# Last dV store but one over fifteen DMA engines, results by GpSimd, second dV written in one go

## The chip, the cores and the metric

The kernel runs on one core of a Trainium2 chip. The core has five engines that run side by side: TensorE (PE; its weight loads are listed apart as PEld), VectorE (DVE), ScalarE (ACT), GpSimd (POOL) and SyncE (SP, which here only issues DMAs). Sixteen DMA engines move data between the main memory (HBM) and the on-chip memory (SBUF, 128 partitions). SP, ACT and GpSimd can each issue DMAs; each has its own queue, and all of them are served by the same sixteen DMA engines. The metric is device time in microseconds (us) of one execution: 644.63 us, the median of three (643.6 to 645.44).

## The reference

One decoding step of attention and its gradient. There are 32 heads; each has one query row, 8192 key rows and 8192 value rows of 128 numbers, all bfloat16.

```
scores = einsum('bhqd,bhkd->bhqk', q, k) * D**-0.5
attn   = softmax(scores)
out    = einsum('bhqk,bhkd->bhqd', attn, v)
```

The outputs are `out` and, by the vector-Jacobian product with `grad_out`, dq, dk and dv. With one query row, dV is the outer product of the softmax weights p and the row of `grad_out`; dK is the outer product of ds = scale · p · (V·grad_out − sum) and the row q. So K and V are read once (67 MB each), and dK and dV, as large as they are, are written: 134.23 MB read and 134.23 MB written by the profile. `out` and dq are 8 KB each.

## The kernel before, in words

**Tiles.** The 32 heads go in `HP` = 16 pairs, t = 0 to 15. One pair's K (or V) is a tile of 128 partitions by 128 rows of 128 numbers, 32 KB a partition, 4 MB in all. There are three buffers for K (`Kt`, K[t] in buffer t mod 3) and two for V (`Vt`). dK and dV are written in place over K and V (`outer`, L325, on DVE: eight operations per tile, one for each eighth of the rows) and are then stored from there (`store`, L335, always issued by SP). A load into a buffer can therefore start only when the store out of it has landed.

**Loads and stores.** `load` (L78 to L81) and `store` (L335 to L339) issue on SP's queue, in program order. A transfer of 4 MB is one DMA of 128 rows of 32 KB, eight rows for each of the sixteen DMA engines. The first and last tiles are moved in quarters or halves.

**Scores of K.** `k_block(t, c)` (L181) takes one eighth of K[t]: DVE transposes it in 32 by 32 blocks (L184), PE multiplies it by the query's columns (L192). Eight blocks make the scores of one pair; DVE and ACT make the softmax of them (`s_back`, `s_top`, `s_exp`, `p_of`).

**Scores of V.** `v_part(t, m)` transposes V on PE (L253), ACT copies it out (L259), `v_scores` multiplies (L270).

**The order.** The program is written out by hand (`tc.manual_schedule()`): every engine executes its instructions in the order in which the Python calls come. The loop over t at L373 does in each pass, in this order on DVE: the dK of pair t−1 (`dk`, eight outer products, stored when done), with the softmax of pair t between them; then the dV of pair t (`outer(t, "p", r)`, r = 0 to 7). From r = 3 on, one block of K of the next pair follows each outer product (L445 to L450). After r = 7 dV is stored (L452; for the first and the last pair in quarters, L447), then come the three last K blocks with the first parts of V (L453 to L456), the load of K[t+2] (L460) and of V[t+2] (L462). At t = 16 only the dK of pair 15 is left, stored in quarters.

**The results.** After the loop `result` (L341) transposes `out` and dq on PE, copies them on ACT and stores each with one DMA of 32 rows of 256 bytes, issued by ACT (L348).

**Semaphores of the DMAs.** Each DMA signals its landing on one of eight semaphores (100, 102, 103, 104, 105, 108, 109 and 110 in the trace), which are handed out in turn to the DMAs of SP and ACT together. Before a DMA takes a semaphore whose last user went through other work, its queue waits until that user has landed. Near the end the turn was: V[14]'s store 103, the first result 104, the first half of dK[14] 105, the second result 108, the second half of dK[14] 109, the four quarters of dV[15] 110, 100, 102 and 103, and the four quarters of dK[15] 104, 105, 108 and 109.

Of the kernel before, what the change touches and what calls it, by code (L numbers as in the profile page):

```python
# [11 lines left out]
BF16 = mybir.dt.bfloat16  # L12
F32 = mybir.dt.float32
# [14 lines left out]
def kernel(  # L28
# [11 lines left out]
    nc = tc.nc  # L40
    P = 128
    _, H, S, D = k.shape
    HP = H // 2
    NT = 2 * S // P
# [15 lines left out]
    small = ctx.enter_context(tc.tile_pool(name="small", bufs=2))  # L60
# [12 lines left out]
    Vt = {t: v_in[t % V_BUFS] for t in range(HP)}  # L73

    def rows_of(x, t, a, b):
        return x[0, 2 * t:2 * t + 2].rearrange("h s d -> (h s) d").rearrange("(p n) d -> p n d", p=P)[:, a:b, :]
# [6 lines left out]
    def load_k(t, parts=1):  # L83
        load(k, Kt, t, parts)
# [96 lines left out]
    def k_block(t, c):  # L181
        x = st[t]
        X = xkpool.tile([P, BN, NW, QD], F32, tag="XK", name="XK_sb")
        nc.vector.transpose(X[:], Kt[t][:, c * BN:(c + 1) * BN, :].rearrange("p n d -> p (n d)").bitcast(F32).rearrange(  # L184
            "p (n w j) -> p n w j", n=BN, w=NW))
        if c == 0:
            x["s"] = psS.tile([P, 512], F32, tag="s", name="s_ps")
        cols = X[:].rearrange("p n w i -> p (n w i)").bitcast(BF16).rearrange(
            "p (n w i e) -> p w e n i", n=BN, w=NW, e=2)
        for w in range(NW):  # L190
            for e2 in range(2):
                nc.tensor.matmul(x["s"][:], lhsT=q_win[:, 2 * w + e2, SL - 1 - c:SL - 1 - c + P],  # L192
                                 rhs=cols[:, w, e2], start=(c == 0 and w == 0 and e2 == 0),
                                 stop=(c == NB - 1 and w == NW - 1 and e2 == 1), skip_group_check=True)

    def s_back(t):
        x = st[t]
        x["sT"] = backs.tile([P, BN, QD], F32, tag="back", name="sT")
        nc.vector.transpose(x["sT"][:].rearrange("p n r -> p (n r)"), x.pop("s")[:])  # L199

    def s_top(t):
        x = st[t]
        mx = small.tile([P, 1], F32, tag="mx")
        nc.vector.reduce_max(mx[:], x["sT"][:, :, 0:NB], axis=AX.XY)
        top = small.tile([P, 1], F32, tag="top")
        nc.vector.tensor_scalar_mul(top[:], mx[:], scale)
        nc.tensor.transpose(x["m"][:, 128:256], top[:].to_broadcast([P, P]), ident_f[:])  # L207

    def s_exp(t):
        x = st[t]  # L210
        nbias = small.tile([P, 1], F32, tag="nbias")
        for s in range(2):
            a, b = s * HF, (s + 1) * HF
            nc.vector.tensor_reduce(nbias[a:b], x["m"][a:b, 128 + a:128 + b], axis=AX.X, op=ALU.max, negate=True)
        e = x["e"] = single.tile([P, NT], F32, tag="e", name="e")
        rs = small.tile([P, 1], F32, tag="rs")
        nc.scalar.activation(e[:].rearrange("p (c n) -> p n c", c=NB), x["sT"][:, :, 0:NB], ACT.Exp, bias=nbias[:],
                             scale=scale, accum_out=rs[:])
        return rs

    def s_sum(t, rs):
        nc.tensor.matmul(st[t]["m"][:, 0:1], lhsT=same[:], rhs=rs[:], start=True, stop=True, skip_group_check=True)  # L222
# [38 lines left out]
    def v_scores(t, z):  # L261
        x = st[t]
        cols = x.pop(("XV", z)).rearrange("p m s -> p (m s)").bitcast(BF16).rearrange(
            "p (m s e) -> p e m s", s=P, e=2)
        if z == 0:
            x["dp"] = psD.tile([P, 512], F32, tag="dp", name="dp_ps")
        at = SL - 2 - 2 * z
        for e2 in range(2):
            for b in range(NQ):
                nc.tensor.matmul(x["dp"][b * QD:(b + 1) * QD, :], lhsT=do_win[:, b // 2, e2, at:at + QD],  # L270
                                 rhs=cols[:, e2, :, b * QD:(b + 1) * QD],
                                 start=(z == 0 and e2 == 0), stop=(z == NZ - 1 and e2 == 1), skip_group_check=True)
# [52 lines left out]
    def outer(t, which, r):  # L325
        x = st[t]
        X, row = (Kt[t], 0) if which == "ds" else (Vt[t], 1)
        a, b = r * BN, (r + 1) * BN
        nc.vector.tensor_tensor(  # L329
            X[:, a:b, :].rearrange("p n (a b) -> p n a b", b=R),  # L330
            x[which][:, a:b, :].unsqueeze(2).to_broadcast([P, BN, D // R, R]),
            x["qd"][:, row, :].rearrange("p (a b) -> p a b", b=R).unsqueeze(1).to_broadcast([P, BN, D // R, R]),
            op=ALU.mult)

    def store(t, which, parts=1, last=None):  # L335
        X, dst = (Kt[t], out_2) if which == "ds" else (Vt[t], out_3)
        L = NT // parts
        for c in (range(parts) if last is None else (last,)):
            nc.sync.dma_start(rows_of(dst, t, c * L, (c + 1) * L), X[:, c * L:(c + 1) * L, :])  # L339

    def result(src, dst):  # L341
        half = single.tile([P, H], BF16, tag="ds1", name="half")
        nc.scalar.copy(half[:], src[:])
        fin_ps = psT.tile([P, 2 * TB, P], BF16, tag="T", name="fin_ps")
        nc.tensor.transpose(fin_ps[0:H, 0, :], half[:], ident[:])
        fin_sb = small.tile([H, D], BF16, tag="qd", name="fin_sb")
        nc.scalar.copy(fin_sb[:], fin_ps[0:H, 0, :])
        nc.scalar.dma_start(dst.rearrange("b h s d -> (b h s) d"), fin_sb[:])  # L348

    NV = NZ * NM // TB  # L350

    def v_part(t, m):
        v_bank(t, m)
        v_copy(t, m)

    HALF = NB // 2
# [16 lines left out]
    for t in range(HP + 1):  # L373
        o = t - 1
        now, old = t < HP, t > 0
        parts = 4 if o == HP - 1 else 2 if o == HP - 2 else 1

        def dk(a, b):
            for r in range(a, b if old else a):
                outer(o, "ds", r)  # L380
                if (r + 1) % (NB // parts) == 0:
                    store(o, "ds", parts, r * parts // NB)

        dk(0, 2)
        if now:
            if old:
                v_part(t, 3)
                v_part(t, 4)
            s_back(t)
            s_top(t)  # L390
            if old:
                v_scores(t, 0)
                v_part(t, 5)
                v_part(t, 6)
        dk(2, 3)
        if now:
            rs = s_exp(t)
            if old:
                for m in (7, 8, 9):
                    v_bank(t, m)  # L400
            s_sum(t, rs)
            if old:
                v_copy(t, 7)
                v_copy(t, 8)
        dk(3, 4)
        if now:
            p_of(t)
            if old:
                v_copy(t, 9)
                v_scores(t, 1)  # L410
                v_part(t, 10)
                v_part(t, 11)
                contract(t, "p")
                v_part(t, 12)
                v_part(t, 13)
                v_scores(t, 2)
                v_part(t, 14)
                v_part(t, 15)
                v_scores(t, 3)
            else:  # L420
                contract(t, "p")
            if old and t + 1 < HP:
                weights_do(t + 1)
        dk(4, NB)
        if not now:
            break
        fine = t == 0 or t == HP - 1
        outer(t, "p", 0)
        outer(t, "p", 1)
        if fine:  # L430
            store(t, "p", 4, 0)
        v_back(t)
        pd_sum(t)
        if t % ST == 0 and old:
            gather(o, "ds")
        outer(t, "p", 2)
        ds_of(t)
        contract(t, "ds")
        if t % ST == ST - 1:
            gather(t, "p")  # L440
        if t + 1 < HP:
            prepare(t + 1)
        else:
            gather(t, "ds")
        for r in range(3, NB):  # L445
            outer(t, "p", r)
            if fine and r % 2:  # L447
                store(t, "p", 4, r // 2)
            if t + 1 < HP and r >= HALF - 1:
                k_block(t + 1, r - HALF + 1)  # L450
        if not fine:
            store(t, "p")  # L452
        if t + 1 < HP:  # L453
            for c in range(HALF + 1, NB):
                k_block(t + 1, c)
                v_part(t + 1, c - HALF - 1)  # L456
            if t + 2 < HP:
                weights_q(t + 2)
        if 0 < t and t + 2 < HP:
            load_k(t + 2)  # L460
        if t + 2 < HP:
            load_v(t + 2, 4 if t == 0 else 1)  # L462
# [34 lines left out]
```

## Time and profile before

| what | value |
|---|---|
| median of three runs | 644.63 us (643.6 to 645.44) |
| the profiled execution's own time | 645.34 us |
| its span, first to last instruction | 643.5 us |
| DVE busy | 503.4 us, 78% |
| PE busy | 448.9 us, 70% |
| ACT busy | 196.0 us, 30% |
| POOL busy | 4.4 us, ten instructions, all before 5 us |
| DMA, SP's queue (q1) | 268.45 MB, 98.1% of sixteen engines' span |
| mean rate over the span | 418 GB/s |
| issue to landing of 4 MB: K load, V load, dK store, dV store | 19.9, 19.3, 29.0, 20.8 us |

The span is cut into 40 slices of 16.1 us on the page. In the sixth slice (80 to 97 us) the rate is 320 GB/s, in the first 353 and in the last two 373 and 269; in the others from the seventh on it lies between 411 and 440 GB/s. The trace also keeps one record for each packet of a DMA and sixteen landing marks for each DMA, one from each DMA engine. It doesn't say which of the sixteen engines a mark or a packet belongs to.

POOL issues no DMA in this kernel.

### The profile page before, as it was taken

The numbers are of one execution on the slowest core, as the hardware profiler recorded it, in microseconds if no ns is written. First come the engines' busy times: TensorE is split into PE (matmuls) and PEld (weight loads), VectorE is DVE, ScalarE is ACT, GpSimd is POOL, SyncE is SP. The second block draws the span as 40 slices with busy tenths as digits, with TensorE's granted clock in tenths as the row PEclk, the third lists the DMA queues.
The fourth block names the chain that finished last, engine by engine and source line by source line (L and its number), as shares of the span: only waits on it lengthen the run. The fifth ranks groups of instructions, "written<-read, shape, count | busy, mean of one in ns | idle before, by whom it ended". The sixth has DMA issues, their size and how long they took to land.

```text
span 643.5 us, 8005 instructions
## 1 busy us (share of the span) xinstructions
PE 448.9 (70%) x3256; PEld 240.5 (37%) x3256; DVE 503.4 (78%) x608; ACT 196.0 (30%) x456; POOL 4.4 (1%) x10
## 2 busy tenths in 40 slices
PE   6768777776868577585785948759687594874840
PEld 6225343442525234153351513416344161431530
DVE  3688999978969599595986959868597695977991
ACT  6113333340604206052060521505215060240610
POOL 2000000000000000000000000000000000000000
PEclk9868798876959779696797987858689695887965
DMA  8999979999999999999999999999999999999986
GB/s 353 431 446 395 439 320 422 420 425 438 435 423 436 429 432 426 430 433 433 428 429 440 428 427 434 431 415 431 417 436 425 431 423 418 437 429 411 424 373 269
DMA packets 12180, 268.97 MB, mean 418 GB/s; under 512 B 1520, under 2 KB 1520, under 8 KB 1520
## 3 DMA queue, kind: packets, MB, share of 16 engines
q1 hardware_dynamic: 12000, 268.45, 98.1%
q8 instruction: 25, 0.41, 0.2%
q14 instruction: 11, 0.09, 0.0%
q10 hardware_dynamic: 144, 0.02, 0.0%
HBM read 134.23 MB, written 134.23 MB: 417 GB/s over the span
## 4 chain that ended last, share of the span: by engine, by line
DMA 44%; DVE 27%; PE 12%; issue 10%; ACT 3%; SPq 1%; DVEq 0%; ACTq 0%
DMA K<-in_k_dram 37%; DVE XK_sb L184 17%; DVE K L329 5%; DMA out_dram<-K 5%; PE T_ps L253 4%; PE s_ps L192 4%; DVE V L329 3%; DMA out_dram<-V 3%; ACT XV_sb L259 2%; PE dp_ps L270 2%; DVE sT L199 1%; PE acc_p L309 1%; PE m_ps L207 1%; SPq L81 1%; ACT p_rep L235 0%
## 5 line engine op out<-in xcount | busy, mean ns | idle before, releaser
L192 PE MATMUL s_ps<-XK_sb,q_win 128*128 128x512 bf16 x512 | 170.7, 471 | 94.8 <-DVE XK_sb L184 93.7
L184 DVE STREAM_TRANSPOSE XK_sb<-K 128x1024 f32<-128x1024 f32 x128 | 152.8, 1223 | 91.3 <-DMA K<-in_k_dram 91.0
L259 ACT COPY XV_sb<-T_ps 128x512 f32<-128x512 f32 x240 | 130.3, 590 | 285.1 <-PE T_ps L253 284.7
L329 DVE TENSOR_TENSOR V<-p_rep,qd 128x2048 bf16<-128x2048 bf16 x128 | 152.1, 1201 | 2.0 <-PE acc_p L309 2.0
L329 DVE TENSOR_TENSOR K<-ds_rep,qd 128x2048 bf16<-128x2048 bf16 x128 | 149.9, 1213 | 0.5
L253 PE MATMUL T_ps<-ident_f,V 128*128 128x128 f32 x1024 | 137.0, 281 | 0.0
L253 PEld LDWEIGHTS T_ps<-ident_f,V 128*128 128x128 f32 x1024 | 116.0, 143 | 38.1 <-issue 9.8
L192 PEld LDWEIGHTS <-q_win 128*128 128x128 bf16 x512 | 57.3, 113 | 191.5 <-issue 167.5
L309 PE MATMUL acc_ds<-K,win_ds 128*32 128x512 bf16 x512 | 55.1, 606 | 27.7 <-ACT win_ds L228 27.7
L270 PE MATMUL dp_ps<-XV_sb,do_win 128*32 128x512 bf16 x480 | 37.2, 383 | 12.6 <-ACT XV_sb L259 11.6
L309 PEld LDWEIGHTS <-win_ds 128*32 128x32 bf16 x512 | 17.2, 134 | 52.5 <-ACT win_ds L228 27.1
L309 PE MATMUL acc_p<-V,win_p 128*32 128x512 bf16 x512 | 32.3, 396 | 3.7 <-ACT win_p L228 1.9
L170 ACT CAST qd<-m_ps 128x256 bf16<-128x256 f32 x16 | 6.0, 372 | 48.3 <-PE m_ps L166 48.1
L228 ACT COPY win_ds<-ds 64x128 bf16<-64x128 bf16 x32 | 9.5, 296 | 36.1 <-DVE ds L296 35.9
L309 PEld LDWEIGHTS <-win_p 128*32 128x32 bf16 x512 | 12.7, 99 | 18.6 <-ACT win_p L228 5.4
L289 PE MATMUL m_ps<-pd,same 128*128 128x1 f32 x32 | 6.2, 264 | 18.7 <-DVE m_ps L283 18.7
L270 PEld LDWEIGHTS <-do_win 128*32 128x32 bf16 x512 | 11.0, 94 | 19.8 <-issue 16.4
L280 DVE STREAM_TRANSPOSE dpT<-dp_ps 128x512 f32<-128x512 f32 x16 | 11.5, 717 | 4.8 <-PE dp_ps L270 4.8
L289 PEld LDWEIGHTS m_ps<-pd,same 128*128 128x128 f32 x32 | 4.9, 191 | 27.1 <-DVE m_ps L283 27.1
L199 DVE STREAM_TRANSPOSE sT<-s_ps 128x512 f32<-128x512 f32 x16 | 11.4, 711 | 4.4 <-PE s_ps L192 4.4
L233 DVE RECIPROCAL rinv<-m_ps 128x1 f32<-128x1 f32 x16 | 2.7, 168 | 13.7 <-PE m_ps L222 13.7
L235 ACT ACTIVATE p_rep<-e,rinv 128x512 bf16<-128x512 f32 x16 | 11.9, 746 | 0.9 <-DVE rinv L233 0.9
(61 smaller groups left out, 158.7 us busy)
## 6 DMA issues: line engine op xcount, KB each, us to landing
K<-in_k_dram SPq DMA_DIRECT2D x15, 4096.0 KB, 19.9
V<-in_v_dram SPq DMA_DIRECT2D x14, 4096.0 KB, 19.3
out_dram<-K SPq DMA_DIRECT2D x14, 4096.0 KB, 29.0
out_dram<-V SPq DMA_DIRECT2D x14, 4096.0 KB, 20.8
V<-in_v_dram SPq DMA_DIRECT2D x8, 1024.0 KB, 9.7
out_dram<-V SPq DMA_DIRECT2D x8, 1024.0 KB, 14.5
K<-in_k_dram SPq DMA_DIRECT2D x4, 1024.0 KB, 16.3
out_dram<-K SPq DMA_DIRECT2D x2, 2048.0 KB, 14.7
```

Source lines behind the costliest of these rows:

```text
L184: nc.vector.transpose(X[:], Kt[t][:, c * BN:(c + 1) * BN, :].rearrange("p n d -> p (n d)").bitcast(F32).rearrange("p (n w j) -> p n w j", ...
L192: nc.tensor.matmul(x["s"][:], lhsT=q_win[:, 2 * w + e2, SL - 1 - c:SL - 1 - c + P], rhs=cols[:, w, e2], start=(c == 0 and w == 0 and e2 == 0),
L199: nc.vector.transpose(x["sT"][:].rearrange("p n r -> p (n r)"), x.pop("s")[:])
L228: nc.scalar.copy(win[which][a:b, :, at + 4 * s:at + 4 * s + 4], src[a:b].rearrange("p (g j) -> p g j", j=4))
L235: nc.scalar.activation(x["p"][:], x["e"][:].unsqueeze(2).to_broadcast([P, NT, R]), ACT.Copy, scale=rinv[:])
L253: nc.tensor.transpose(T_ps[:, j, :], words[:, at * P:(at + 1) * P], ident_f[:])
L259: nc.scalar.copy(x["XV", z][:, i * TB:(i + 1) * TB, :], x.pop(("T", m))[:])
L270: nc.tensor.matmul(x["dp"][b * QD:(b + 1) * QD, :], lhsT=do_win[:, b // 2, e2, at:at + QD], rhs=cols[:, e2, :, b * QD:(b + 1) * QD], start ...
L280: nc.vector.transpose(dpT[:].rearrange("p m r -> p (m r)"), x.pop("dp")[:])
L289: nc.tensor.matmul(x["m"][:, 1:2], lhsT=same[:], rhs=x["pd"][:], start=True, stop=True, skip_group_check=True)
L309: nc.tensor.matmul(acc[which][b * QD:(b + 1) * QD, :], lhsT=win[which][:, g, at:at + QD], rhs=X[:, 4 * g:4 * g + 4, :].rearrange("p n d -> ...
L329: nc.vector.tensor_tensor(X[:, a:b, :].rearrange("p n (a b) -> p n a b", b=R), x[which][:, a:b, :].unsqueeze(2).to_broadcast([P, BN, D // ...
```

## The change

Three edits:

1. dV[14], the last pair but one, is stored by `store_spread`. GpSimd first issues a tiny DMA of five rows (`turn`, two numbers a row, into a small tile that nothing reads) and then one DMA of the partitions 0 to 119, 120 rows of 32 KB. SP issues the partitions 120 to 127 as two DMAs of four rows. The name of the change says that the 120 rows go over fifteen DMA engines, and that the tiny DMA turns the cursor from which GpSimd's DMAs are dealt out.
2. The two results are issued by GpSimd instead of ACT.
3. In the pass t = 1 no K block stands between the outer products of dV[1]; all eight outer products come first, then dV[1]'s store, then the blocks 0 to 4 of K[2], and then blocks 5 to 7 as before.

```
+    def store_spread(t):
+
+        turn = small.tile([P, 1], F32, tag="mx", name="turn")
+        nc.gpsimd.dma_start(turn[0:5].bitcast(BF16).unsqueeze(2), q[0, 0:5].rearrange("h s d -> (h s) d")[:, 0:4].rearrange(
+            "h (a b) -> h a b", b=2)[:, :, 0:1])
+        nc.gpsimd.dma_start(rows_of(out_3, t, 0, NT)[0:120], Vt[t][0:120], max_dma_last_dim=16384)
+        for a in (120, 124):
+            nc.sync.dma_start(rows_of(out_3, t, 0, NT)[a:a + 4], Vt[t][a:a + 4])
+
     def result(src, dst):
...
-        nc.scalar.dma_start(dst.rearrange("b h s d -> (b h s) d"), fin_sb[:])
+        nc.gpsimd.dma_start(dst.rearrange("b h s d -> (b h s) d"), fin_sb[:])
...
-            if t + 1 < HP and r >= HALF - 1:
+            if t + 1 < HP and t != 1 and r >= HALF - 1:
                 k_block(t + 1, r - HALF + 1)
-        if not fine:
+        if t == HP - 2:
+            store_spread(t)
+        elif not fine:
             store(t, "p")
+        if t == 1:
+            for c in range(HALF + 1):
+                k_block(t + 1, c)
         if t + 1 < HP:
             for c in range(HALF + 1, NB):
                 k_block(t + 1, c)
```

## The prediction

> **What bounds the kernel now.** I read the DMA rows first, then SP's queue in time, then windows, and last the landing marks.
>
> ```profile
> q1 hardware_dynamic: 12000, 268.45, 98.1%
> q8 instruction: 25, 0.41, 0.2%
> 523.37 0.34 SPq L81 DMA_DIRECT2D K<-in_k_dram  x1
> 563.02 0.34 SPq L81 DMA_DIRECT2D K<-in_k_dram  x1
> 592.07 0.34 SPq L339 DMA_DIRECT2D out_dram<-V  x1
> 602.74 6.31 SPq L339 DMA_DIRECT2D out_dram<-K  x2
> 610.99 9.43 SPq L339 DMA_DIRECT2D out_dram<-V  x4
> 627.68 5.80 SPq L339 DMA_DIRECT2D out_dram<-K  x4
> ```
>
> Columns of the lower rows are start, duration, queue, line and transfer. The DMA engines (I call each a lane) are busy 98.1% of the span, so compute is under cover and only lane time counts. A packet of 32 KB takes 1.21 us (median of the packet records), so eight packets, one lane's share of 4 MB, take 9.7 us and the four transfers of a pair 38.7. The K loads come 39.65 us apart. The missing 0.93 us is the second row: 25 packets of 16 KB of the program itself, 1.5 per pair, each worth half a 32 KB packet, 0.61 us; 1.5 × 0.61 = 0.92. That fits only if one lane gets them all. The landing marks say the same: of the sixteen marks of one DMA the last is 1.7 us behind the median for K[1]'s load (landed 34.5 us) and 6.7 us for V[14]'s store (median 606.2, fifteenth 607.9, sixteenth 612.9). Since loads wait for the slow lane's landing, the other lanes cannot run further ahead, and from some 400 us on the slow lane sets the pace. Its sum: after 85 us 56 shares of 4 MB are left (64 less eight), 56 × 9.7 = 543, plus 22 × 0.61 = 13, together 556 us; from 85.1 to its last landing at 642.66 are 557.5. It is never idle.
>
> ```profile
> 82.00:84.50 2.50, 1.04 (x4) 0.38 (x4) 2.50 (x3) 0.00 (x0) 0.00 (x0) 1.00 0.06 26
> 84.50:85.10 0.60, 0.00 (x0) 0.00 (x0) 0.60 (x1) 0.00 (x0) 0.00 (x0) 1.00 0.00 0
> 624.00:627.50 3.50, 0.00 (x0) 0.00 (x0) 3.50 (x4) 0.00 (x0) 0.00 (x0) 0.50 0.47 197
> 627.50:630.50 3.00, 0.00 (x0) 0.00 (x0) 1.64 (x2) 0.26 (x1) 0.00 (x0) 0.50 0.73 300
> 638.80:642.30 3.50, 0.00 (x0) 0.00 (x0) 0.00 (x0) 0.00 (x0) 0.00 (x0) 0.50 0.06 26
> ```
>
> The last two numbers of a window are the DMA share and GB/s. 0.06 is one lane of sixteen: in the last 3.5 us a single lane works. Around 625 us the fifteen others starve, and from 82 to 85 us all do.
>
> ```profile
> SPq L339 <- DMA out_dram<-fin_sb: 11.3, 2, 7.2
> 627.69 0.26 ACT L347 COPY fin_sb<-fin_ps 32x128 bf16<-32x128 bf16 x1 [4.31 <-DMA out_dram<-fin_sb]
> ```
>
> SP waited for the results' landings before it stored dK[15]: the first quarter shares semaphore 104 with the first result (landed 627.62), the third 108 with the second (632.59).
>
> **Second dV in one go.** dV[1]'s last product ends at 84.2 us because four blocks stand between the products.
>
> ```profile
> 75.12 1.24 DVE L184 STREAM_TRANSPOSE XK_sb<-K 128x1024 f32<-128x1024 f32 x1
> 77.39 1.24 DVE L184 STREAM_TRANSPOSE XK_sb<-K 128x1024 f32<-128x1024 f32 x1
> 79.65 1.24 DVE L184 STREAM_TRANSPOSE XK_sb<-K 128x1024 f32<-128x1024 f32 x1
> 81.91 1.24 DVE L184 STREAM_TRANSPOSE XK_sb<-K 128x1024 f32<-128x1024 f32 x1
> ```
>
> Each costs 1.13 us of pitch, so the store leaves SP 4.5 us earlier, 79.8 instead of 84.28, before dK[0]'s store has left any lane (first lane 81.7, slow lane 84.5 by the packet records). The slow lane then saves its idle time from 84.5 to the first packet at 85.1 to 85.3: **0.7 us**. The others save some 3.5 us, which are lost again, as they may not run ahead. Behind the store in SP's queue stands K[3]'s load, which needs dK[0]'s landing at 84.9 and went at 84.97; it stays. The moved blocks end at the same 88.7 on DVE; PE takes 1.03 us for a block's four products (83.20 row: 1.04), less than DVE's 1.13, so it ends some 1 us after DVE as before. Cost zero, under cover of K[2]'s later work; without the cover a microsecond.
>
> **dV[14] off the slow lane.** The transfer's size is unchanged. If the lane left out is the slow one, its work shrinks by eight packets, 9.7 us: 642.66 − 0.7 − 9.7 = 632.3, and it no longer ends last. No row names the slow lane, so the relief lies between 0 and 9.7 us; I take 9.7, since its marks make it the one lane for which fifteen-lane dealing makes sense at all, and keep 0 as a rival. SP's eight rows are eight packets; two DMAs of four rows put one packet each on at most four lanes, twice: between 0.6 (spread evenly, 9.7/16) and 2.4 us (2 × 1.21) more on some lanes. I take 2.4, four rows being unable to reach more than four lanes at a packet a row.
>
> GpSimd's issue has no row. SP's takes 0.85 us from issue (84.28) to first packet (85.12). The store leaves DVE at 592.07 and the first lane is done with what stands before it (dK[13], first mark) at 595.8, so up to 3.7 us are hidden; beyond that each microsecond is one lost. I take zero; the far end is the rival below. The tiny DMA is ten numbers; it waits only for an old buffer of the row maximum, free since pair 13's softmax, so it stands ahead of the store by tens of microseconds. On POOL's queue nothing else waits; on SP's, dK[14]'s first half is behind the two small stores, 2 × 0.34 us, and went 10 us later anyway. Nobody waits for dV[14]'s landing but the end.
>
> **Results by GpSimd.** The two result DMAs leave the turn of eight semaphores, the extra small store enters it. By the turn, dK[15]'s quarters then follow users that land by 618 us, so they leave SP when DVE has made them: products at 619.98 in steps of 1.14, so 622.3, 624.6, 626.9 and 629.1 instead of 627.68 to 633.07. ACT's second copy waits for the first result (4.3 us), off the path: the second result may land as late as 636. For the slow lane alone this part is worth nothing (it was never starved); with the slow lane relieved it is worth the 3.5 us that the fifteen others starve.
>
> **Sum.** dV[15]'s last quarter lands on the fifteen lanes at 625.0 to 627.4, median 625.8. Shifted by 0.7: 624.3 to 626.7. Four quarters of dK[15] without a gap, 4 × 2.44 = 9.8. The four lanes with two more rows: 2.4. So these end at 636.5 to 638.9 by where they stand among the fifteen; I take 638.0, over the middle because the latest of four counts. Compute does not bind: the last quarter leaves at 628.4 and needs 3.3. The last landing moves by 642.66 − 638.0 = 4.7. The profiled execution took 645.34 (span 643.5 and 1.84 around it), 0.71 above the median; 645.34 − 4.7 = 640.6, so **640.0** by the median of 644.63. Own range 638.4 to 641.0.
>
> **Rivals.**
> - The lane left out is not the slow one: all lanes but it are as before, only 0.7 us is won: 643.9. For it: the trace names no lane, and a cursor can stand elsewhere. Against it: nothing in rows. If the slow lane is even one of the four with two more rows: 643.9 + 2.4 = 646.3. Chances 0.15 and 0.04. [...]
> - The other side: the GpSimd store itself is slow, through late issue, or because rows taken in blocks of eight, and four rows next to each other, crowd one way out of SBUF. Price: nothing up to a second 9.7 us on fifteen lanes (pace halved), or up to 2 × 3 × 1.21 = 7.3 on four (four packets one after the other instead of at once). It decides at 4.7 us, where the gain is gone: 644.6; at the far end 640.0 + 9.7 = 649.7. For it: every transfer that runs at 430 GB/s here has 128 rows on all lanes; no row shows another. Against it: a lane works on two queues at once (the 16 KB program packets took 0.95 us beside data), so dK[13] and dK[14], in the other queue, fill what a slow packet leaves. Chance 0.20: 0.07 of it so that the end lies within 0.3% of before, 0.13 slower. [...]
>
> **Chances.** As forecast 0.61. 0.3% (1.9 us) is about what a measurement of this kernel can tell from none. Faster: 0.61. Within: 0.15 + 0.04 + 0.07 = 0.26. Slower: 0.13. The range from 638.3 to 646.3 leaves out the slow store's far end and little else.
>
> **What would show it.** Right: the store of dV[1] leaves SP at 79.8 and the window 82 to 85 us has a DMA share near 1; dK[15]'s quarters leave at 621.6 to 628.4; at the end no window of share 0.06, and the sixteenth mark of dK[15] is within 3 us of the median. Wrong: one lane still alone for 3 us at the end (another lane freed); marks of the GpSimd store or the small ones 10 us and more behind their turn (slow store); SP still waiting for results.

## The result and the profile after

The changed kernel takes 649.8 us (median of 4 runs, 649.13 to 650.29) against 644.12 us for the kernel before on the same chip: ratio 1.0086, 95% interval 1.0064 to 1.0107, so 5.7 us slower. I had forecast 640.0 in a range of 638.3 to 646.3. The profiled execution took 649.72 us, its span 647.9.

First the DMA queues of the changed kernel by the page (packets, MB, share of sixteen engines' span), SP's queue and POOL in time, and one row of the DMA issues between 588 and 626 us (size, us to landing):

```profile
q1 hardware_dynamic: 11872, 264.52, 96.4%
q0 software_dynamic: 368, 3.95, 2.0%
...
588.07 1.13 SPq L348 DMA_DIRECT2D out_dram<-V  x2
598.73 6.34 SPq L339 DMA_DIRECT2D out_dram<-K  x2
606.99 10.74 SPq L339 DMA_DIRECT2D out_dram<-V  x4
618.36 9.34 SPq L339 DMA_DIRECT2D out_dram<-K  x4
...
588.35 0.77 POOL L346 DMA_DIRECT2D out_dram<-V  x1 [70.68 <-DVE V L329]
...
out_dram<-V POOLq DMA_DIRECT2D x1, 3840.0 KB, 35.6
```

GpSimd's queue is q0. Its 240 data packets of 16 KB (the 120 rows came out as two packets each) took 0.84 us in the mean of the packet records, together the 2.0% of 16 × 647.9 us; the 256 packets of 16 KB of dK[14]'s halves took 0.61 in the kernel before (median). The store needed 35.6 us to land, where SP's store of the whole tile took 20.8 before. Everything up to it was early: dV[14] left at 588.07 instead of 592.07, and the first quarter of dK[15] at 618.36 instead of 627.68. These nine microseconds of head start were lost between there and the end.

Windows, with the DMA share and GB/s as the last two numbers, show where. The first line is the kernel before, the others are the changed kernel:

```profile
602.00:624.00 22.00, 15.61 (x146) 10.07 (x143) 20.59 (x25) 9.67 (x25) 0.00 (x0) 0.81 0.99 422
...
82.00:84.50 2.50, 2.50 (x8) 0.87 (x7) 1.80 (x3) 0.00 (x0) 0.00 (x0) 0.63 1.00 433
...
592.00:600.00 8.00, 7.27 (x63) 5.21 (x61) 6.90 (x12) 5.15 (x12) 0.00 (x0) 1.00 0.90 255
600.00:612.00 12.00, 8.14 (x97) 4.56 (x94) 11.58 (x16) 6.18 (x14) 0.00 (x0) 0.90 1.01 311
612.00:624.00 12.00, 6.48 (x42) 4.29 (x34) 12.00 (x12) 1.41 (x6) 0.53 (x1) 0.50 0.99 389
624.00:636.00 12.00, 0.00 (x0) 0.00 (x0) 1.14 (x2) 0.25 (x1) 0.52 (x1) 0.50 0.96 401
636.00:640.00 4.00, 0.00 (x0) 0.00 (x0) 0.00 (x0) 0.00 (x0) 0.00 (x0) 0.50 0.64 270
640.00:643.00 3.00, 0.00 (x0) 0.00 (x0) 0.00 (x0) 0.00 (x0) 0.00 (x0) 0.50 0.27 112
643.00:646.40 3.40, 0.00 (x0) 0.00 (x0) 0.00 (x0) 0.00 (x0) 0.00 (x0) 0.50 0.13 53
```

The row from 82 us is the stretch that stood at a share of 0.06 before; it is full now. From 592 to 612 us the lanes are as busy as ever (0.90 and 1.01) but move 255 and 311 GB/s. Against the 422 GB/s of the first line that is 8 × 167 + 12 × 111 + 12 × 33 = 3064 KB less by 624 us (1 GB/s times 1 us is 1 KB), or 7.3 us of DMA time. The end is ragged: in the last 3.4 us the share is 0.13, two lanes. The sixteen landing marks of dK[15]'s last quarter run from 631.25 to 646.92. The sign of a slow store that the prediction named is there: the GpSimd store landed 35.6 us after its issue, 15 us more than SP's.

### The profile page after: what moved, and what is told of

Same layout as the page of the kernel before. It is cut to its first block, busy times and chain, and to the rows that moved or that the text cites. A ratio compares the mean times of both kernels' runs of the same rounds, so it can differ in the third digit from the quotient of the medians.

```text
span 647.9 us, 8009 instructions
## 1 busy us (share of the span) xinstructions
PE 440.1 (68%) x3256; PEld 236.8 (37%) x3256; DVE 503.6 (78%) x608; ACT 195.7 (30%) x456; POOL 6.9 (1%) x14
## 4 chain that ended last, share of the span: by engine, by line
DMA 45%; DVE 26%; issue 11%; PE 11%; ACT 4%; SPq 1%; POOLq 0%; POOL 0%; DVEq 0%; ACTq 0%
DMA K<-in_k_dram 36%; DVE XK_sb L184 16%; DMA out_dram<-K 8%; DVE K L329 4%; PE T_ps L253 4%; PE s_ps L192 3%; DVE V L329 3%; ACT XV_sb L259 2%; PE dp_ps L270 2%; DVE sT L199 1%; PE acc_p L309 1%; PE m_ps L207 1%; ACT p_rep L235 1%; PE m_ps L321 1%; PE acc_ds L309 1%
## 5 line engine op out<-in xcount | busy, mean ns | idle before, releaser
L192 PE MATMUL s_ps<-XK_sb,q_win 128*128 128x512 bf16 x512 | 165.4, 457 | 98.6 <-DVE XK_sb L184 97.3
L253 PE MATMUL T_ps<-ident_f,V 128*128 128x128 f32 x1024 | 135.6, 279 | 0.4 <-ACT K L259 0.4
L253 PEld LDWEIGHTS T_ps<-ident_f,V 128*128 128x128 f32 x1024 | 114.4, 142 | 38.3 <-issue 8.2
L192 PEld LDWEIGHTS <-q_win 128*128 128x128 bf16 x512 | 56.0, 110 | 191.9 <-issue 165.2
L309 PEld LDWEIGHTS <-win_p 128*32 128x32 bf16 x512 | 12.7, 99 | 18.6 <-ACT win_p L228 5.4
## 6 DMA issues: line engine op xcount, KB each, us to landing
out_dram<-V SPq DMA_DIRECT2D x8, 1024.0 KB, 20.8
```

The source lines that it names most:

```text
L253: nc.tensor.transpose(T_ps[:, j, :], words[:, at * P:(at + 1) * P], ident_f[:])
L309: nc.tensor.matmul(acc[which][b * QD:(b + 1) * QD, :], lhsT=win[which][:, g, at:at + QD], rhs=X[:, 4 * g:4 * g + 4, :].rearrange("p n d -> ...
```

## The experiments

Theory 1: lane 4, the one left out, is the slow lane, and the relief came; but rows that stand next to each other in SBUF crowd, and what they lose is more than the relief. Theory 2: a wrong lane was freed. Theory 3: GpSimd's queue itself is slow.

The runs come from several chips, on which the median of the kernel before was 643.51 to 644.69 us; a difference between runs of different chips is good to about a microsecond.

### The parts by themselves

`e1_dv2_results` has the second dV in one go and the results by GpSimd; `store_spread` and its call are not there.

> dV[14] goes as before, in one store of 128 rows by SP; the second dV in one go and the results by GpSimd stay. If the whole loss sits in dV[14]'s store, this kernel is 0.7 us below the one before (the slow lane's idle stretch at 85 us): about 643.4; the quarters of dK[15] leave SP as soon as DVE has made them (622 to 629 us), the fifteen other lanes end at about 635, and the slow lane works alone for some 7 us at the end. Rival: SP's wait for the results held the end up by itself; then 640 or less. Second rival: the second dV in one go or GpSimd's result DMAs cost something of their own; then over 645.

641.75 us against 643.51 (10 and 13 runs), ratio 0.9972 (0.9963 to 0.9981): 1.8 us faster.

```profile
618.40 7.14 SPq L339 DMA_DIRECT2D out_dram<-K  x4
```

The quarters of dK[15] leave at 618.4 to 625.2, the fifteen lanes end at 631.1 to 633.8 by the marks and one alone at 638.67, as expected (the lone lane is 4.8 us behind, not 7); but the gain is 1.8 us and not 0.7.

`e2_spread` is the opposite: only the new store.

```
         if t == HP - 2:
             store_spread(t)
         elif not fine:
             store(t, "p")
```

> Only dV[14]'s store is changed (GpSimd 120 rows, SP twice four rows); results by ACT and the second dV mixed, as before. If the loss sits in this store: 650.5 (649.8 and the 0.7 us that the second dV is worth), or up to 653 if SP's wait for the results binds again. If the three parts only harm together: near 644.

651.66 us against 643.51, ratio 1.0139 (1.0104 to 1.0174). The new store alone costs 8.1 us (651.66 − 643.51). In company it costs 649.8 − 641.75 = 8.1 as well, or 5.68 + 1.76 = 7.4 if each is taken against the kernel before on its own chip. All of the loss is in it.

`e8_dv2_only` has the one edit of pass t = 1.

> Only the second dV in one go; results by ACT, dV[14]'s store as before. The two edits together gave -1.76 us. If all of it is the stretch at 85 us (the slow lane's landing of dV[1] came 2.3 us earlier), this kernel alone gives -1.8 us, 641.7. If SP's wait for the results was worth something, it gives 0.7 us or less.

641.34 us against 643.94, ratio 0.9961 (0.9946 to 0.9976). So the second dV gives all that the two edits gave, and the results by GpSimd nothing that can be seen. In its profile the last landing mark of dV[1] is at 94.26 (before 96.36), of V[3]'s load at 114.37 (118.46) and of dK[1] at 124.13 (128.21). The lead grows by 2 us after the idle stretch is over. The first lane's landings show how: dV[1]'s store, K[3], V[3] and dK[1] followed one another in 9.85, 9.53, 9.71 and 9.65 us; in the kernel before, counted from the first packet at 85.12, in 10.54, 10.04, 10.40 and 9.76, 2.0 us more for the same four transfers.

This holds beyond the two profiles. K[3], V[3] and dK[1] together took 30.2 to 30.4 us on the first lane in all five traces whose pass t = 1 is as before (`before`, `e2_spread`, `e4_marks`, `e10_marks_late`, `e12_few_products`), and 28.8 to 29.1 in all nine that write the second dV in one go. In `e2_spread` and `e10_marks_late` the slow lane was never idle: dV[1]'s store left at 81.97 and 81.95, before that lane was done with dK[0] (84.66 and 84.83), and its next mark came one normal share of 9.66 us later. So the idle time that I had counted comes and goes with the execution, and the slower transfers are what all five share. Two stretches hold most of it in the kernel before: 32 KB packets that set out between 92.2 and 94.6 us took 1.56 us in the mean and those between 113.8 and 116.2 us 1.69, instead of 1.21. Why, is open: with the mixed pass most lanes run dry together around 82 us and set off together, but the work of the other engines is shifted too, and no run separates the two. The profiles alone would give a gain of 4.2 us at the end (last landing 638.42 instead of 642.66); the medians give 2.6.

### Which lane is the slow one, and was it freed

`e4_marks` puts a tiny DMA behind most dV stores of the kernel before.

```
             store(t, "p")
+            mark = small.tile([P, 1], F32, tag="mx", name="mark")
+            nc.sync.dma_start(mark[0:t + 1].bitcast(BF16), q[0, 0:t + 1].rearrange("h s d -> (h s) d")[:, 0:2])
```

> The kernel before, with a tiny DMA of n = t + 1 rows (4 bytes each) behind every dV store of the passes 1 to 14 on SP's queue, to see which lane is the slow one: a DMA of n rows should give n late marks, and the other 16 - n at once. If such DMAs run on the lanes 0 to n - 1, the late marks hold one straggler 2 to 7 us behind the rest from one n on, and the slow lane is number n - 1. By the cursor that was turned by five and went on for fifteen, lane 4 is the one that the change left out: the straggler then appears from n = 5 on. If it appears first at another n, the change freed a lane that was not slow. Time: within 1 us of the kernel before.

644.91 us in one run. A DMA of n rows did give n late marks. But the small n fell into the early passes, when the slow lane was less than 2 us behind, and these don't decide: with n = 4 the last mark is 0.9 us behind the one before it, with n = 5 it is 1.6. `e10_marks_late` uses n = 17 − t, so that the small n come late.

> The kernel before with tiny DMAs of n = 17 - t rows behind the dV stores of the passes 8 to 14 (n = 9 down to 3), when the slow lane is 4 to 7 us behind. If lane 4 is the slow one, n = 5 to 9 show a last mark 3 us and more behind the one before it, and n = 3 and 4 show none. If the straggler is gone at another n, the slow lane is that number. Time within 1 us of the kernel before.

643.9 us in one run. The marks of the last five DMAs, in us from the start (the first mark of each, from the lanes that have nothing to do, is left out):

```
n = 7  445.10 445.30 445.52 446.21 446.26 447.36 452.37
n = 6  484.41 484.87 485.44 485.78 488.09 492.04
n = 5  524.44 524.63 524.67 524.75 531.85
n = 4  564.21 564.36 564.53 564.75
n = 3  604.21 604.25 604.62
```

With five rows one lane comes 7.1 us behind the one before it, with four rows none. So the straggler is the fifth, number 4 counted from 0, if a DMA of n rows takes the first n lanes of one fixed order; these marks fit that (straggler with n = 5, 6 and 7, none with n = 3 and 4), and no run here contradicts it.

`e3_no_turn` is the changed kernel without the tiny DMA of five rows:

```
-        turn = small.tile([P, 1], F32, tag="mx", name="turn")
-        nc.gpsimd.dma_start(turn[0:5] ...
```

> The changed kernel without the tiny DMA ahead of the store, all else the same, so another lane should be left out. If the changed kernel did free the slow lane (theory 1: the relief came, crowding ate it), the slow lane here carries its eight rows again and ends 10 us later than in the changed kernel, at 643 or later, and the time is 650 to 655. If the tiny DMA does nothing, or the changed kernel freed a wrong lane (theory 2), the time is 649.8 within 1 us or falls, and the end looks alike.

653.5 us against 643.51, ratio 1.0143 (1.0115 to 1.0171). In its profile (656.6 us, the slowest of the four runs) the last two of the sixteen marks of dK[15]'s fourth quarter are 649.47 and 653.79: one lane alone, 4.3 us behind all others. In the changed kernel the last two marks are 646.71 and 646.92 and nobody is alone. So the tiny DMA did turn the dealing, and with it the straggler is gone: the changed kernel did free lane 4. Theory 2 falls.

### Why the store is slow

`e5_gpsimd_128_rows` lets GpSimd store all 128 rows, and SP none:

```
-        nc.gpsimd.dma_start(rows_of(out_3, t, 0, NT)[0:120], Vt[t][0:120], max_dma_last_dim=16384)
-        for a in (120, 124):
-            nc.sync.dma_start(rows_of(out_3, t, 0, NT)[a:a + 4], Vt[t][a:a + 4])
+        nc.gpsimd.dma_start(rows_of(out_3, t, 0, NT), Vt[t][:], max_dma_last_dim=16384)
```

> The changed kernel, but GpSimd's store takes all 128 rows of dV[14] and SP's two small stores are gone: GpSimd's issue alone, no lane left out. Theory 1 (rows in blocks crowd): if GpSimd deals 128 rows as SP does, its 16 KB packets take 0.61 us, as at full pace, and the time is that of the kernel with the two other edits alone, 641.75, plus at most 2 us for the late start (first packet 3.1 us after the issue instead of 0.85). Rival (GpSimd's queue itself is slow): packets of 0.86 us mean as in the changed kernel and about 650.

641.68 us against 643.94, ratio 0.9969 (0.9957 to 0.998), the same as without any GpSimd store (641.75). Its queues on the page, and the windows that were slow in the changed kernel:

```profile
q1 hardware_dynamic: 11856, 264.25, 96.9%
q0 software_dynamic: 368, 4.21, 1.6%
...
592.00:600.00 8.00, 7.27 (x62) 5.21 (x60) 6.90 (x13) 5.15 (x12) 0.00 (x0) 1.00 0.99 423
600.00:612.00 12.00, 8.15 (x94) 4.57 (x94) 11.58 (x16) 6.07 (x13) 0.00 (x0) 0.89 0.99 422
```

Its 256 packets of 16 KB took 0.62 us in the mean of the packet records, the pace of the kernel before (0.61), at 422 GB/s. GpSimd's queue, its 16 KB packets and its late first packet (3.1 us after the issue) cost nothing. Theory 3 falls.

`e7_sp_120_rows` has the 120 rows issued by SP and no tiny DMA:

```
-        nc.gpsimd.dma_start(rows_of(out_3, t, 0, NT)[0:120], Vt[t][0:120], max_dma_last_dim=16384)
+        nc.sync.dma_start(rows_of(out_3, t, 0, NT)[0:120], Vt[t][0:120])
```

> The changed kernel with the 120 rows issued by SP instead of GpSimd (no tiny DMA), the eight rows as in the change. SP's DMA of 120 rows should go over fifteen lanes too, but lane 15 is then the one left out, not the slow one. If rows in blocks of eight crowd whoever issues them, packets of 32 KB take 2 us and more in place of 1.21 and the time is over 650, like the kernel without the tiny DMA (653.5), in which the slow lane was not freed either. If GpSimd's queue is the cause, the time is 643 to 645.

658.66 us against 643.94, ratio 1.0228 (1.0213 to 1.0243), the worst of all. Its windows:

```profile
592.00:600.00 8.00, 7.33 (x59) 5.39 (x57) 7.35 (x11) 4.46 (x10) 0.00 (x0) 1.00 1.00 284
600.00:612.00 12.00, 8.09 (x93) 4.68 (x96) 11.13 (x16) 6.94 (x15) 0.00 (x0) 0.95 0.98 255
```

The same slowness with another issuer: busy lanes, 255 to 284 GB/s. The 32 KB packets between 588 and 630 us took 1.83 us in the mean instead of 1.21. The tiny DMAs of SP reached the slow lane from n = 5 on (`e10_marks_late`), so by my estimate 120 rows by SP do not free lane 4 either, and the run to compare with is `e3_no_turn`: 653.5 with GpSimd issuing, 5.2 us less. That what SP issues next has to stand behind the slow store is a likely reason for these, not a shown one.

`e9_sp_halves` takes the odd numbers away: SP stores dV[14] as two DMAs of 64 rows.

```
+        for a in (0, 64):
+            nc.sync.dma_start(rows_of(out_3, t, 0, NT)[a:a + 64], Vt[t][a:a + 64])
```

> The changed kernel, but dV[14] is stored by SP as two DMAs of 64 rows, partitions 0 to 63 and 64 to 127: all 16 lanes, four packets each and DMA, no lane left out, nothing by GpSimd. [...] If the odd number of lanes or the four-row pieces did the harm, packets stay at 1.21 and the time at 641.7.

654.45 us against 644.08, ratio 1.0156 (1.0127 to 1.0184); 12.7 us above the 641.75 of one store of 128 rows, with the same rows, bytes, issuer and sixteen lanes. That is more than the 9.7 us that the prediction put as the far end of a slow store. 32 KB packets took 2.0 us in the mean between 588 and 630 us instead of 1.21. The window 592 to 600:

```profile
592.00:600.00 8.00, 7.70 (x65) 5.35 (x63) 6.90 (x13) 5.40 (x12) 0.00 (x0) 1.00 1.05 267
```

So a store can become slow with all sixteen lanes, by how its rows are split over DMAs, and the issuer does not decide it: 267 GB/s here, nearly all of it before dK[14] left SP at 598.54, where 128 rows in one DMA gave 423 by either issuer (SP in `e8_dv2_only`, GpSimd in `e5_gpsimd_128_rows`). Why the split does this was not shown: no trace says which rows the lanes read at the same time, and that neighbouring rows crowd is my estimate. For the 120 rows of the change the same cause is argued, not shown: no run moves 120 rows over sixteen lanes, so the rows and the fifteen lanes are not separated there. Theory 1 is the one that is left, with this reservation.

`e6_no_small_stores` leaves SP's two stores of four rows out of the changed kernel.

> The changed kernel without SP's two stores of four rows: the last eight partitions of dV[14] are left unwritten, 256 KB of 268 MB. If the two lanes that end 4 us behind all others are held up by those eight rows (four packets of 32 KB took 6 to 8 us instead of 1.21, twice), the end falls from 649.8 to the level of the rest, about 645.5. If the 120 rows alone do the harm, it falls by less than 1.5 us.

647.49 us against 643.94, ratio 1.0053 (1.0035 to 1.0072), so 2.3 us below the changed kernel and 5.8 above `e5_gpsimd_128_rows` on the same chip. This lies between the two expectations: the 120 rows do the greater part, the eight rows the rest. The 120 rows are slow by themselves:

```profile
q0 software_dynamic: 368, 3.95, 2.4%
...
592.00:600.00 8.00, 7.99 (x61) 5.64 (x58) 6.76 (x10) 4.45 (x10) 0.00 (x0) 0.96 0.99 247
600.00:612.00 12.00, 8.08 (x93) 4.70 (x96) 11.10 (x16) 6.95 (x15) 0.00 (x0) 0.90 0.97 279
```

GpSimd's packets took 1.03 us in the mean here, and the two lanes that ended 4 us behind the rest in the changed kernel (646.71 and 646.92, the next at 642.78) are gone: the last marks are 641.56, 642.82 and 643.03. In the changed kernel the four lanes' marks of the first small store came at 597.7 to 600.4 and those of the second at 601.6 to 606.6; the first four packets set off at 591.4 to 592.3 and took 5.9 to 7.6 us, not 1.21.

### Relief in small portions

`e11_thin` starts from the second dV in one go and gives each dV from pass 2 to 14 an eighth of its row (4 KB) by GpSimd over fifteen lanes, with tiny DMAs (five rows, then eight and nine) that are to make GpSimd's dealing leave out the same lane each time, and the last eight partitions' eighth by SP.

```
+        nc.gpsimd.dma_start(rows_of(out_3, t, CUT, NT)[0:120], Vt[t][0:120, CUT:NT, :], max_dma_last_dim=16384)
+        nc.sync.dma_start(rows_of(out_3, t, 0, CUT), Vt[t][:, 0:CUT, :])
+        nc.sync.dma_start(rows_of(out_3, t, CUT, NT)[120:P], Vt[t][120:P, CUT:NT, :])
```

> The kernel before with the second dV in one go, and from pass 2 to 14 the last eighth of each dV row (4 KB) goes by GpSimd over fifteen lanes, lane 4 left out each time, the rest by SP on all lanes: 1.2 us of relief for the slow lane in each pass, 15.7 in all, against 0.9 us that the program packets cost it. If crowding costs only where nothing else is queued, the transfers in SP's queue fill it and the time falls to 636 to 639. If crowding costs what it costs in the changed kernel whatever stands beside it (about as much lane time as is moved), the fifteen others lose 1 us per pass, and the time is 641 to 646.

651.86 us against 644.08, ratio 1.0125 (1.0093 to 1.0156); 10.5 us above the kernel with the second dV alone. The relief itself shows: late in the run the last mark of SP's 4 MB transfers is mostly within a microsecond of the one before it, where it was 3 to 5.5 us behind in the kernel before, though the sixteen marks still spread over 6 to 9 us. But the K loads now come 40.1 to 41.0 us apart late in the run, before 39.65: some 0.8 us more in each of thirteen passes, 10 us in all. That is above my second expectation. The portions themselves did not crowd: their 4 KB packets took 0.16 us, next to an eighth of 1.21. What became slower are SP's 32 KB packets, 1.26 us in the mean between 408 and 570 us instead of 1.23 in `e8_dv2_only`, which makes most of the 0.8 us a pass. Why, this run does not tell; three further small DMAs a pass stand in the queues as well.

### Does the program's own traffic make lane 4 slow

`e12_few_products` leaves 28 of the 32 products of each contraction out of the kernel before.

> The kernel before with 28 of the 32 products of each contraction left out (L309, in both contractions of all sixteen pairs), so that the results are sums over an eighth of the rows and wrong; dK, dV and all DMAs of data stay. PE then runs 896 products and as many weight loads fewer, 1792 instructions, some seven of the 25 program packets. If these packets are what makes lane 4 the slow one and lane 4 sets the pace, the end comes 7 x 0.61 = 4.3 us earlier: 639.5 against 644 for the kernel before, with DVE's and SP's work the same. If the slow lane is slow for another reason (its place, its part of SBUF), the time stays within 0.3%.

```
-        for g in range(first, last):
+        for g in range(first, NQ):
```

641.41 us against 644.69, ratio 0.9955 (0.994 to 0.997): 3.3 us faster where I expected 4.3. The page's row for the program packets fell from 25 to 18 as expected:

```profile
q8 instruction: 18, 0.29, 0.2%
```

But the run does not settle it. In its profile dK[1] landed 2.5 us earlier than in the kernel before (125.71 against 128.21); in `e10_marks_late`, with all products, it was 2.0 us (126.20), so fewer packets are not needed for that. From there to the last landing took 513.3 us. In five traces with all 25 packets and dV[14] in one DMA of SP (`before`, `e4_marks`, `e10_marks_late`, `e8_dv2_only`, `e1_dv2_results`) it took 514.3 to 515.3, so six packets fewer are worth 1.0 to 2.0 us, 0.16 to 0.33 each and not 0.61. The last eleven K loads were 39.46 us apart in the mean, before 39.52. So lane 4's lag is not explained by these packets alone; what the rest is stays open.

## Why the prediction was wrong

**Lane 4 sets the pace: right.** The marks name one straggler, and leaving it out removes it from the end (`e3_no_turn`, `e10_marks_late`). That the program packets are the whole reason is not borne out (`e12_few_products`). The sum that spoke for it took 39.65 us between K loads; this holds for the last of them, and the mean of the last eleven is 39.52.

**Second dV, 0.7 us: right way, wrong source.** It measured 2.6 us alone (0.9961) and 1.8 us in company (0.9972). I counted only lane 4's idle time, which two other traces of the same order do not have; the transfers behind dV[1]'s store run slower in that order, some 1.4 us for three of them in every trace, and this I had not seen. The moved blocks cost nothing that shows, as I said.

**The new store: this step failed.** I took 9.7 us of relief on lane 4, which came, and in the sum set the price of moving the rows by blocks at zero, with 9.7 us as its far end. The sum let the fifteen other lanes end at 638.0; they ended at 646.92, and with the store of 128 rows they end at 633.83 (`e1_dv2_results`), so the price was 13.1 us on them, the 2.4 that I had given the eight rows included. The relief could return only 4.8 of it (lane 4 alone at 638.67 against 633.83), and the net loss measured 7.4 to 8.1 us. My reason for zero was that dK[13] and dK[14], in the other queue, fill what a slow packet leaves. Between 592 and 612 us they did not: dK[13] was over on most lanes at 592.8, dK[14] left SP only at 598.73, and what ran beside the slow packets became slow too, at 311 GB/s from 600 to 612 us with dK[14] in the queue. Lane 4 shows it best: it had none of the 120 rows, yet it needed 14.2 us (588.56 to 602.78) for dK[13]'s eight packets, where 9.7 are normal. By the packet records they followed one another without a pause; the first five took 1.21 to 1.27 us, the last three 2.43, 3.47 and 2.05. What held them up was not shown. Of the 9.7 us that the relief took from this lane, 4.5 were lost again in dK[13]'s slower packets.

**The eight rows, 2.4 us.** Without them the kernel is 2.3 us faster, but not for the reason that I gave: they did not take two packets' time of 1.21 us on four lanes. The first four packets took 5.9 to 7.6 us, and the marks of the second four came another 3.9 to 6.6 us later, part of it beside other work. That the sizes agree is luck.

**GpSimd's issue at zero: right.** First packet 3.1 us after the issue, inside the 3.7 us of cover; 128 rows by GpSimd cost nothing (641.68 against 641.75).

**Results by GpSimd: right as far as it was put to the test.** SP no longer waits for them and the quarters leave 8 to 9 us earlier (`e1_dv2_results`), but `e1_dv2_results` and `e8_dv2_only` differ by 0.4 us the wrong way, within their intervals. ACT's second copy waited 7.25 us for the first result, off the path, as predicted. The last quarter did wait in the changed kernel until 627.36, for the semaphore of dK[14]'s second half, which landed late because of the new store; I had not reckoned with that.

**The rival.** The slow store was named, with the row that spoke for it (no transfer at 430 GB/s had other than 128 rows). I gave its slower part 0.13 and left it out of the range; an overlap that no run had measured outweighed that row. That its far end, 649.7, meets the measured 649.8 is luck in part: the far end was 2.4 + 9.7 = 12.1 us on the fifteen lanes, 13.1 were measured, and without the store these lanes would have ended 1.8 us before where I put them (633.83 against 638.0 − 2.4).

The version to keep is `e8_dv2_only`, 641.34 us, below both kernels; with the two results by GpSimd it is the same within the intervals.

## What to carry to other kernels

Before moving rows from one DMA engine to others, ask which rows each DMA covers: here a 128-row store ran at 422 GB/s, while with 120 or 64 rows at a time the stream fell to some 250 to 310 GB/s with the lanes marked busy (0.90 to 1.05). Do not count on transfers in another queue to fill the loss before a run has shown that they do. Read the rate beside the busy share: from 600 to 612 us the changed kernel's lanes were marked busy at 1.01 and moved 311 GB/s. Bringing one store forward was worth more here (2.6 us) than the idle time of the slowest lane that it closes (0.7 in the forecast, none in two other traces), so compare the transfers behind a gap too, in more than one trace.

## What the runs showed of the hardware

- With two stores of 64 rows the kernel took 12.7 us longer than with one of 128 rows and the same bytes (654.45 in `e9_sp_halves` against 641.75 in `e1_dv2_results`).
- One DMA engine fell behind in the kernel before: the last mark of dV[15]'s fourth quarter came at 632.89, 5.5 us after the one before it and 7.1 after the median. A tiny DMA of n rows from SP gave n late marks, and late in the run the straggler was among them from n = 5 on (7.1 us behind at n = 5, none at n = 4, `e10_marks_late`).
- An engine that had no part in the slow store took 14.2 us for eight packets of 32 KB beside it in the changed kernel (588.56 to 602.78), where eight packets of 1.21 us are 9.7.
- In the pass in which most or all lanes ran dry between 82 and 85 us, the three transfers of 4 MB after dV[1]'s store took 30.2 to 30.4 us on the first lane in five traces, instead of 28.8 to 29.1 in nine in which they did not. The cause is open.
- GpSimd's DMA put its first packet out 3.1 us after the issue (588.35 to 591.49 in the changed kernel), SP's 0.85 (84.28 to 85.12 in the kernel before), and GpSimd's rows of 32 KB, with `max_dma_last_dim=16384` in the call, came out as packets of 16 KB.
